# A longer distance between attention's matmuls and their operands in a planned schedule, with the steady part's ranks replaced

## The chip, the core and the metric

The kernel runs on one core of one Trainium2 chip. The metric is device time in microseconds, from repeated executions; one more execution is taken with the hardware profiler, and all rows below come from that one.

## What is computed

Attention with pooled keys and values, and behind it a feed-forward network with a PReLU. Cut to what matters:

```python
# q, k, v: (8, 8, 576, 64)   w_in: (512, 2048)   w_out: (2048, 512)   alpha: (2048,)
k_p = k.reshape(B, H, 72, 8, D).mean(axis=3)
v_p = v.reshape(B, H, 72, 8, D).mean(axis=3)
scores = np.matmul(q, k_p.transpose(0, 1, 3, 2)) / np.sqrt(D)
attn = softmax(scores)                      # over the 72 pooled keys
x = np.matmul(attn, v_p).transpose(0, 2, 1, 3).reshape(4608, 512)
h = x @ w_in
g = np.maximum(h, 0.0) + alpha * np.minimum(h, 0.0)
return g @ w_out
```

All of it is float32. The kernel forms each float32 product from float16 halves: an operand is scaled by a power of two and split into a high and a low part, and three matmuls (low x high, high x low, high x high) make one product.

## The kernel before

**Tiling.** The 4608 tokens go in nine chunks of 512 (c = 0 to 8). A chunk has attention (four tiles of 128 tokens), the first FFN matmul (FFN1, 512 to 2048 features), the PReLU, and the second (FFN2, 2048 to 512). Chunk 0 and attention of chunk 1 belong to the start, which has a plan and constants of its own (RK). The steady part follows: FFN of chunks 1 to 8 and, one chunk ahead of it, attention of chunks 2 to 8. FFN1 of chunk 1 is a plain product (lines 1339 to 1341). From chunk 2 on it is a Winograd form of Strassen's product (the function fast, line 1368): seven products in place of eight on sums of quarters, in four blocks d for each chunk, with three PSUM banks x, y and z that ACT (line 1384) and DVE (line 1388) empty into SBUF between the products. FFN2 is plain for chunks 1 and 2 (lines 1575 to 1577), and half Winograd from chunk 3 on (ffn2s, line 1481). DVE, ACT and GpSimd do the PReLU (lines 1325, 1327) and the splits into halves (lines 854, 857, and 1438 to 1450 for the sums that FFN2's products need; the step at 1450 gives back a buffer that the next copy of line 1384 takes).

**Attention of a chunk** (the function ahead). k, q and v are loaded by SP's DMA queue (lines 1028, 1039, 1076); DVE sums k and v over eight rows (1030, 1078). The largest absolute value gives a scale: reduce_max has ACT or GpSimd spread the partitions' maxima over a diagonal (lines 259 and 261), one small matmul bring them to all partitions (line 265, called the bring here), and DVE take the maximum. ACT and DVE split q, k and v. Then, for each of four tiles: a scores matmul (line 651), a maximum, a subtraction, an exponential, a sum and a reciprocal (1122 to 1127, 304, 306), GpSimd's multiplication (1131), copies into the padded tile apad (1133 to 1138), and a transposing DMA into aT (1142). After two tiles each comes a mix, the product with v (line 661), whose result is split into x (1169 to 1198). A chunk's first scores also wait for the first FFN1 block of the chunk before (gate). There is one S bank of PSUM, one e tile and one apad for all of it.

**What sets the order.** Every step is given to a planner, `_Plan.add`, with its engine, an estimated duration, the steps that it comes after, a rank, and the slots that it takes and gives (`take`, `give`: buffers and banks). `emit` simulates the engines in time and writes the instructions in the order found; each engine then runs its own in that order, and semaphores guard the data. A step may start, for the planner, when its engine is free, its slots are free, and its operands are there:

```python
t = [self.free.get(op["engine"], 0.0)]
t += [d["end"] + op["slack"] for d in op["after"] if self.loose < 1 or d["engine"] != op["engine"] or d["engine"] == "SP"]
```

So `slack`, the distance, is added to the end of each operand that another engine makes (loose is 1), and not to slots. The end of a step has 0.13 us added for the hop between engines, a DMA 2.0 (HOP, DMA_HOP). Of the steps of an engine that could start within a short time of the first (NEAR: 0.05 us on DVE, 0.18 on ACT, 0.37 on GpSimd, 0.07 on PE) the one with the lowest rank goes. A rank is 1000 times the chunk plus a constant of the table RB: `top` for the evacuations of Winograd's banks, `late`, `last`, `pr` and `gp` for PReLU and splits, `f1s`, `f2`, `f2s` and `f2o` for FFN products, and for attention `ld` (q), `k`, `v`, `t0` to `t3` (tiles), `x` and `y` (mixes). A name with `_` is the same for chunk 2. Attention of chunk c + 1 has 1000 c as its base, as the FFN of chunk c has.

The distances: 0.2 for attention's steps by default, FAR = 0.6 for its scores (line 1115), its mixes (line 1164) and the matmuls that sum weights (line 1242, whose operands are PE's own), 0.3 for Winograd products and 0.1 for plain FFN2 products. The bring has the default.

Of the kernel before, what the change touches and what calls it, by code (L numbers as in the profile page):

```python
# [56 lines left out]
def _new_b(c):  # L57
# [10 lines left out]
          ld1=13695.5, ld1s=7460.7, one=0, vl=6947.7, ld2=6076.4, q0=-19570.2, v0=1372.2, sm0=-8437.5,  # L68
          sms0=1712.0, mix0=-2376.7, q1=6121.6, v1=8243.2, sm1=3009.5, sms1=2826.1, mix1=16889.9)

RB = dict(gate=0, ld=4164.3, k=3254.6, v=4232.2, t0=-10914.8, t1=-12652.6, t2=-1841.8, t3=-12650.9, x=-4876.9,
          y=-10807.7, sum=-2021.0, pl=-18854.5, pp=5227.9, top=-10886.6, late=-13984.8, last=12811.0,
          pr=-12701.6, gp=11083.2, f2=7996.3, w1=-21973.2, sg=-4791.0, top2=-11574.2, f2o=1648.1, sum2=-1841.6,
          sums=1092.3, a2=-16165.4, ld_=1931.9, k_=-9571.1, v_=-13979.9, t0_=1665.0, t1_=-4791.7, t2_=-13992.2,
          t3_=2394.1, x_=-22301.6, y_=1604.9, sum2s=-10358.3, f2s=37.7, f1s=1612.4, out=2429.2)

# [103 lines left out]
def pooled_attention_prelu_ffn(ctx: ExitStack, tc: tile.TileContext, qT, kT, vT, vN, w1, w2, alpha, out):  # L182
# [14 lines left out]
    gp = ctx.enter_context(tc.tile_pool(name="gp", bufs=16))  # L197
# [34 lines left out]
    sg = const.tile([P, NF], F32, name="sg")  # L232
# [395 lines left out]
    last, scaled, pooled_v = {}, {}, []  # L628
# [331 lines left out]
    with tc.manual_schedule(engines={ENG.SP, ENG.PE, ENG.DVE, ENG.Activation, ENG.Pool}):  # L960
        plan = start()
# [24 lines left out]
        ld=[ldp.tile([P, KH], F32, tag="ld", name="ld") for _ in range(2)],  # L986
# [10 lines left out]
    def held(kind, tile_):  # L997
        box = _Box(kind)
        box.slot = tile_
        return box  # L1000
    add, FAR = plan.add, 0.6
    NQ = NF // 4
    pairs = lambda d: [(d, j) for j in range(2)]
    tw = {p: pieces[n] for n, p in enumerate(p for d in range(NS) for p in pairs(d))}
# [5 lines left out]
    def ahead(c, rank):  # L1010
        bs, n, at = _new_b(c), [0], ["ld"]

        def add(*a, **k):
            n[0] += 1
            return plan.add(*a, **{"slack": 0.2, **k, "rank": rank + RB[at[0] + "_" * (c == 2)] + 0.001 * n[0]})
        kss = {b: _Box("f", lambda t: t[:, :NPR * SP].rearrange("p (a s) -> p a s", s=SP)) for b in bs}
        m = once(lambda: sml.tile([P, 4], F32, tag="m", name="m"))
        e = once(lambda: sml.tile([P, 4], F32, tag="e", name="e", bufs=4))
# [6 lines left out]
        for j, b in enumerate(bs):  # L1025
            for i in range(2):
                t = _Box("ld")
                x = add("SP", 1.65, lambda i=i, b=b, t=t: nc.sync.dma_start(out=t(), in_=kT[b, :, i * KH:i * KH + KH]),
                        take=t)
                done.append(add("DVE", 1.3, lambda i=i, b=b, t=t: nc.vector.tensor_reduce(  # L1030
                    out=kss[b]().rearrange("p a s -> p (a s)")[:, i * KH // POOL:(i + 1) * KH // POOL],
# [6 lines left out]
        for i in range(2):  # L1038
            x = [add("SP", 1.46, lambda i=i: nc.sync.dma_start(out=q[i](), in_=qT[c, i]), *x, take=q[i])]
# [12 lines left out]
        for j, b in enumerate(bs):  # L1052
# [3 lines left out]
                out=kbs[b % 2][:, :, 1], in0=kss[b](), scalar=s()[:, j + 2:j + 3], in1=kbs[b % 2][:, :, 0],  # L1056
                op0=ALU.mult, op1=ALU.subtract), h, give=kss[b], two=True))
        for i in range(2):
            h = add("ACT", 1.13, lambda i=i: nc.scalar.activation(
                q16s[c][i]()[:, 0], q[i](), AF.Copy, scale=s()[:, 1 - i:2 - i]), sc)  # L1060
            for j in range(2):
                ps_ = slice(2 * j, 2 * j + 2)
                h = add("DVE", 0.7, lambda i=i, ps_=ps_: nc.vector.scalar_tensor_tensor(
                    out=q16s[c][i]()[:, 1, ps_], in0=q[i]()[:, ps_], scalar=s()[:, 1 - i:2 - i],
# [6 lines left out]
        for b in bs:  # L1071
            vs = _Box("f", lambda t: by_head(t[:SP]))
            ps = []
            for i in range(4):
                t = _Box("ld", lambda t: t[:SP, :2 * D * POOL].rearrange("p (a d w) -> p a d w", a=2, w=POOL))
                x = add("SP", 0.82, lambda i=i, b=b, t=t: nc.sync.dma_start(out=t(), in_=vT[b, :, 2 * i:2 * i + 2]),
                        take=t)
                ps.append(add("DVE", 1.15, lambda i=i, t=t, vs=vs: nc.vector.tensor_reduce(  # L1078
                    out=vs()[:, 2 * i:2 * i + 2, :], in_=t(), axis=AX.X, op=ALU.add), x, *ps[-1:],
# [5 lines left out]
            x = add("DVE", 0.65, lambda vm=vm, vs=vs: absmax(vm()[:SP], vs().rearrange("p h d -> p (h d)")), z, *ps)  # L1085

            def vscale(t, w, b=b, vsc=vsc):
# [3 lines left out]
            x = reduce_max(add, lambda vm=vm: vm(), 1, vscale, 0.3, x, home=_Box("S"))  # L1091
            x = add("ACT", 0.72, lambda v16=v16, vs=vs, vsc=vsc: nc.scalar.activation(
                v16()[:SP, 0], vs(), AF.Copy, scale=vsc()[:SP]), x, take=v16)
            y = add("DVE", 0.73, lambda v16=v16, vs=vs, vsc=vsc: nc.vector.scalar_tensor_tensor(
                out=v16()[:SP, 1], in0=vs(), scalar=vsc()[:SP], in1=v16()[:SP, 0],
                op0=ALU.mult, op1=ALU.subtract), x, give=vs, two=True)
# [8 lines left out]
        for i in range(TPC):  # L1105
# [7 lines left out]
            x = add("PE", 0.56 * len(_parts(c, i)), lambda i=i, ps=ps: scores(c, i, ps()), *kd,  # L1113
                    qd[2 * (i // 2) + 1], *tiles[-1:], *gate.get((c - 1, RB["gate"]), ()),
                    take=(ps, ex), give=q16s[c][i // 2] if i % 2 else (), slack=FAR)
# [4 lines left out]
            def top(i=i, mx=mx, sv=sv):  # L1120
                descale(c, i)
                nc.vector.tensor_reduce(out=mx(), in_=sv(), axis=AX.X, op=ALU.max)
            x = add("DVE", 0.9, top, x)
            x = add("DVE", 0.75, lambda ex=ex, mx=mx, sv=sv: nc.vector.tensor_tensor(
                out=ex(), in0=sv(), in1=mx().broadcast_to([P, 2, 4, SP]), op=ALU.subtract), x, give=ps, slack=0.0)
            x = add("ACT", 0.78, lambda i=i, ex=ex: nc.scalar.activation(ex(), ex(), AF.Exp, scale=descale(c, i)), x)
            x = add("DVE", 0.75, lambda sm=sm, ex=ex: nc.vector.tensor_reduce(
                out=sm(), in_=ex(), axis=AX.X, op=ALU.add), x)

            x = add("DVE", 0.4, lambda i=i: over9(i), x, slack=0.0)  # L1130
            x = add("Pool", 1.15, lambda ex=ex, sm=sm: nc.gpsimd.tensor_tensor(  # L1131
                out=ex(), in0=ex(), in1=sm().broadcast_to([P, 2, 4, SP]), op=ALU.mult), x)
            y = add("ACT", 0.68, lambda ev_=ev_: nc.scalar.copy(out=ap[:, 0, :, :SP], in_=ev_()), x, take="ap")  # L1133
            z = add("SP", 0.5, lambda: nc.sync.dma_start(out=ap[:, 1, :, :SP], in_=ap[:, 0, :, :SP]), y)
            x = add("Pool", 1.0, lambda ev_=ev_: nc.gpsimd.tensor_tensor(  # L1135
                out=ap[:, 0, :, SP:], in0=ev_()[:, :, :LO0], in1=ap[:, 0, :, :LO0], op=ALU.subtract), y)
            w = add("Pool", 0.45, lambda ev_=ev_: nc.gpsimd.tensor_tensor(
                out=ap[:, 1, :, SP:2 * SP - LO0], in0=ev_()[:, :, LO0:], in1=ap[:, 0, :, LO0:SP], op=ALU.subtract),
                y, x, give=ex, slack=0.0)
# [39 lines left out]
        ps, x = halves(0)  # L1179
# [4 lines left out]
        ps, x = halves(1)  # L1184
# [482 lines left out]
```

## Time and profile before

| | |
|---|---|
| median of 3 runs | 824.03 us (823.13 to 824.06) |
| the profiled execution | 823.68 us |
| its span, first to last instruction | 821.9 us |
| granted TensorE clock, mean | 0.994 of full speed |
| busy: DVE | 76% |
| busy: ACT | 58% |
| busy: GpSimd | 51% |
| moved by DMA | 137.98 MB, mean 168 GB/s |

How to read it: shares are of the span. PE is TensorE's matmuls; they are pipelined, so the time in which PE is busy contains the latency of each, and two matmuls that follow each other overlap. Steps of a chain of waits are the work that the end goes back to: each piece is what released the next one. A wait is the idle time of an engine just before an instruction, put down to what released it last. The start, up to about 150 us, includes most of PE's idle time; the steady part is what comes after it.

### The profile page before, as it was taken

The numbers are of one execution on the slowest core, as the hardware profiler recorded it, in microseconds if no ns is written. First come the engines' busy times: TensorE is split into PE (matmuls) and PEld (weight loads), VectorE is DVE, ScalarE is ACT, GpSimd is POOL, SyncE is SP. The second block draws the span as 40 slices with busy tenths as digits, with TensorE's granted clock in tenths as the row PEclk, the third lists the DMA queues.
The fourth block names the chain that finished last, engine by engine and source line by source line (L and its number), as shares of the span: only waits on it lengthen the run. The fifth ranks groups of instructions, "written<-read, shape, count | busy, mean of one in ns | idle before, by whom it ended". The sixth has DMA issues, their size and how long they took to land.

```text
span 821.9 us, 17523 instructions
## 1 busy us (share of the span) xinstructions
PE 788.3 (96%) x7075; PEld 593.4 (72%) x7075; DVE 627.2 (76%) x1070; ACT 480.6 (58%) x824; POOL 417.6 (51%) x412
## 2 busy tenths in 40 slices
PE   6889998989999989999999999999999999999998
PEld 4634444445458745788888888888888888888887
DVE  6999996599978966997799788978886587338710
ACT  5799874566356564566366736664575465526521
POOL 1657854246454554467455626563565365525430
PEclk9989999999999999999999999999999999999999
DMA  9994216447975984775487658674646164425001
GB/s 350 295 318 163 87 47 124 148 160 216 239 238 196 286 227 114 204 243 145 113 221 182 186 143 238 165 185 129 205 143 148 41 208 149 122 56 203 2 26 52
DMA packets 134833, 137.98 MB, mean 168 GB/s; under 512 B 108032, under 2 KB 111168, under 8 KB 134752
## 3 DMA queue, kind: packets, MB, share of 16 engines
q1 hardware_dynamic: 134752, 136.87, 57.3%
q8 instruction: 55, 0.90, 0.4%
q14 instruction: 26, 0.21, 0.1%
HBM read 96.48 MB, written 16.78 MB: 138 GB/s over the span
## 4 chain that ended last, share of the span: by engine, by line
PE 65%; DVE 15%; DMA 9%; ACT 5%; issue 3%; POOL 2%; DVEq 0%; ACTq 0%; POOLq 0%; SPq 0%
PE b L1368 25%; PE b L1481 23%; DMA aT<-apad 5%; PE b L1575 3%; PE b L1577 3%; PE b L1576 3%; PE s L651 1%; PE s L661 1%; DVE w L748 1%; DMA ld<-vT_dram 1%; DVE h L1327 1%; DVE v L720 1%; PE b L1339 1%; PE b L1341 1%; PE b L1340 1%
## 5 line engine op out<-in xcount | busy, mean ns | idle before, releaser
L1368 PE MATMUL b<-x,w 128*128 128x256 f16 x2352 | 271.4, 273 | 1.9 <-ACT h L1384 1.2
L1368 PEld LDWEIGHTS <-w 128*128 128x128 f16 x2352 | 228.4, 98 | 33.1 <-issue 2.1
L1481 PE MATMUL b<-w,g 128*128 128x256 f16 x1584 | 183.8, 273 | 0.6 <-ACT hw L1527 0.6
L1481 PEld LDWEIGHTS <-g 128*128 128x128 f16 x1728 | 168.1, 98 | 21.5 <-issue 1.7
L857 POOL TENSOR_TENSOR g<-h,g 128x512 f16<-128x512 f32 x88 | 107.4, 1232 | 78.1 <-ACT g L854 77.1
L1327 DVE SCALAR_TENSOR_TENSOR h<-h,al 128x512 f32<-128x512 f32 x88 | 73.8, 875 | 9.8 <-ACT h L1325 9.7
L1388 DVE TENSOR_TENSOR h<-b,h 128x512 f32<-128x512 f32 x85 | 58.0, 685 | 22.8 <-PE b L1368 22.1
L1325 ACT ACTIVATE h<-h,rp 128x512 f32<-128x512 f32 x78 | 52.2, 714 | 31.3 <-DVE h L1388 30.7
L854 ACT CAST g<-h 128x512 f16<-128x512 f32 x88 | 52.4, 616 | 20.3 <-DVE h L1327 10.6
L857 POOL TENSOR_TENSOR g<-hw,g 128x512 f16<-128x512 f32 x40 | 47.5, 1199 | 30.3 <-ACT g L854 21.7
L1131 POOL TENSOR_TENSOR e<-e,sum 128x576 f32<-128x576 f32 x28 | 34.4, 1227 | 44.2 <-DVE sum L306 44.0
L1135 POOL TENSOR_TENSOR apad<-e,apad 128x448 f16<-128x448 f32 x28 | 33.3, 1188 | 45.4 <-ACT apad L1133 43.8
L1575 PE MATMUL b<-w,g 128*128 128x512 f16 x128 | 48.6, 380 | 0.0
L1576 PE MATMUL b<-w,g 128*128 128x512 f16 x128 | 48.5, 379 | 0.0
L1577 PE MATMUL b<-w,g 128*128 128x512 f16 x128 | 48.5, 379 | 0.0
L1481 PEld LDWEIGHTS <-sw 128*128 128x128 f16 x396 | 38.6, 98 | 6.3 <-issue 1.7
L1384 ACT COPY h<-b 128x512 f32<-128x512 f32 x39 | 22.5, 578 | 34.4 <-PE b L1368 27.4
L1522 DVE TENSOR_TENSOR h<-b,h 128x512 f32<-128x512 f32 x26 | 17.6, 687 | 32.7 <-PE b L1481 32.5
L1078 DVE TENSOR_REDUCE f<-ld 72x128 f32<-72x1024 f32 x24 | 28.8, 1205 | 11.9 <-DMA ld<-vT_dram 11.8
L1388 DVE TENSOR_TENSOR hw<-b,hw 128x512 f32<-128x512 f32 x40 | 27.3, 684 | 10.6 <-PE b L1368 8.0
L1176 POOL TENSOR_TENSOR x<-h,x 128x512 f16<-128x512 f32 x16 | 19.5, 1230 | 28.7 <-ACT x L1169 28.6
L1481 PE MATMUL b<-sw,sw 128*128 128x256 f16 x264 | 33.0, 273 | 1.1 <-DVE hw L1540 1.1
(282 smaller groups left out, 1553.5 us busy)
## 6 DMA issues: line engine op xcount, KB each, us to landing
w<-b SPq DMA_DIRECT2D x56, 896.0 KB
w<-w_dram SPq DMA_DIRECT2D x16, 1024.0 KB
ld<-vT_dram SPq DMA_DIRECT2D x24, 288.0 KB
ld<-kT_dram SPq DMA_DIRECT2D x12, 576.0 KB
ld<-qT_dram SPq DMA_DIRECT2D x12, 512.0 KB
b<-w SPq DMA_DIRECT2D x8, 512.0 KB
out_dram<-h SPq DMA_DIRECT2D x16, 256.0 KB
apad<-apad SPq DMA_DIRECT2D x28, 144.0 KB
```

What stands on the lines that cost most here:

```text
L854: nc.scalar.copy(out=g[:, 0], in_=t)
L857: nc.gpsimd.tensor_tensor(out=g[:, 1], in0=t, in1=g[:, 0], op=ALU.subtract)
L1131: x = add("Pool", 1.15, lambda ex=ex, sm=sm: nc.gpsimd.tensor_tensor(out=ex(), in0=ex(), in1=sm().broadcast_to([P, 2, 4, SP]), op=ALU.mult ...
L1135: x = add("Pool", 1.0, lambda ev_=ev_: nc.gpsimd.tensor_tensor(out=ap[:, 0, :, SP:], in0=ev_()[:, :, :LO0], in1=ap[:, 0, :, :LO0], op=ALU. ...
L1325: nc.scalar.activation(t, t if src is None else src, AF.Copy, scale=rp[:, f:f + 1])
L1327: nc.vector.scalar_tensor_tensor(out=t, in0=t, scalar=al[:, f:f + 1], in1=t, op0=ALU.mult, op1=ALU.max)
L1368: nc.tensor.matmul(ps[:, q], weights(n, ws[q](), l, k), x[:, r, k], start=begin and not (q or k or e), stop=end and q + k + e == 4, skip_g ...
L1388: nc.vector.tensor_tensor(out=half(*o) if o else z, in0=banks[bank](), in1=z, op=ALU.add)
L1481: nc.tensor.matmul(bank[b]()[:, i], a, w, start=b in fresh, stop=stop, skip_group_check=True)
L1575: nc.tensor.matmul(ps, g[:, 1, ts_], w[:, 0, cs], start=(n == 0), stop=False)
L1576: nc.tensor.matmul(ps, g[:, 0, ts_], w[:, 1, cs], start=False, stop=False)
L1577: nc.tensor.matmul(ps, g[:, 0, ts_], w[:, 0, cs], start=False, stop=(n == NF - 1))
```

## The change

Three edits. The constant FAR goes from 0.6 to 1.8. The default distance of attention's steps stays 0.2 on all engines but PE, where it becomes 1.3; scores and mixes have FAR, so that on PE this is the bring of reduce_max. And the table RB has new values for all its 38 ranks (gate, the block whose end lets the next chunk's scores begin, stays 0). No operation is added or removed, and the start's constants stay.

```diff
-RB = dict(gate=0, ld=4164.3, k=3254.6, v=4232.2, t0=-10914.8, t1=-12652.6, t2=-1841.8, t3=-12650.9, x=-4876.9,
-          y=-10807.7, sum=-2021.0, pl=-18854.5, pp=5227.9, top=-10886.6, late=-13984.8, last=12811.0,
-          pr=-12701.6, gp=11083.2, f2=7996.3, w1=-21973.2, sg=-4791.0, top2=-11574.2, f2o=1648.1, sum2=-1841.6,
-          sums=1092.3, a2=-16165.4, ld_=1931.9, k_=-9571.1, v_=-13979.9, t0_=1665.0, t1_=-4791.7, t2_=-13992.2,
-          t3_=2394.1, x_=-22301.6, y_=1604.9, sum2s=-10358.3, f2s=37.7, f1s=1612.4, out=2429.2)
+RB = dict(gate=0, ld=1986.5, k=2080.0, v=2672.8, t0=-9490.5, t1=1792.0, t2=1603.8, t3=-13535.3, x=2823.5,
+          y=-342.4, sum=-2703.0, pl=880.9, pp=-4455.6, top=-1915.0, late=-3830.3, last=-1198.0, pr=-29472.6,
+          gp=2670.7, f2=9824.2, w1=1082.2, sg=-4068.9, top2=578.1, f2o=-1191.0, sum2=2688.9, sums=1785.4,
+          a2=-32370.0, ld_=10964.6, k_=1355.8, v_=-3660.6, t0_=-1142.8, t1_=-13646.8, t2_=5942.3, t3_=684.4,
+          x_=-13662.5, y_=1979.2, sum2s=-13639.8, f2s=2606.6, f1s=5636.5, out=-35531.5)
...
-    add, FAR = plan.add, 0.6
+    add, FAR = plan.add, 1.8
...
-            return plan.add(*a, **{"slack": 0.2, **k, "rank": rank + RB[at[0] + "_" * (c == 2)] + 0.001 * n[0]})
+            return plan.add(*a, **{"slack": 1.3 if a[0] == "PE" else 0.2, **k, "rank": rank + RB[at[0] + "_" * (c == 2)] + 0.001 * n[0]})
```

## Rows read from the trace of the kernel before

**Rows 1.** The page's busy times: each engine's busy us, share of the span, and instructions.

```profile
PE 788.3 (96%) x7075; PEld 593.4 (72%) x7075; DVE 627.2 (76%) x1070; ACT 480.6 (58%) x824; POOL 417.6 (51%) x412
```

**Rows 2.** Busy time by stretch from 150.2 us to the last matmul, seven stretches and their sum: the stretch and its length, busy us and instructions of PE, PEld (weight loads), DVE, ACT and POOL, the granted clock, the DMA engines' share and GB/s.

```profile
150.20:320.00 169.80, 164.56 (x1234) 96.78 (x1235) 135.97 (x242) 95.11 (x168) 88.37 (x84) 1.00 0.72 209
...
480.00:560.00 80.00, 80.00 (x834) 70.42 (x833) 67.73 (x112) 47.71 (x82) 44.42 (x43) 1.00 0.67 180
...
720.00:818.60 98.60, 97.95 (x902) 87.13 (x899) 44.32 (x70) 37.58 (x67) 31.39 (x28) 1.00 0.20 66
sum 668.40, PE 658.18 PEld 525.80 DVE 499.13 ACT 363.57 POOL 336.84; mean PE 94.03 PEld 75.11 DVE 71.31 ACT 51.94 POOL 48.12
```

**Rows 3.** Who waited for whom, PE alone, from 150.2 us on: us in total, times, the longest.

```profile
PE s L651 <- DVE x L1172: 2.7, 1, 2.7
PE s L265 <- ACT pd L259: 2.3, 1, 2.3
PE s L661 <- DMA aT<-apad: 1.5, 2, 1.3
PE b L1368 <- ACT h L1384: 1.2, 1, 1.2
PE b L1481 <- DVE hw L1540: 1.1, 1, 1.1
PE b L1481 <- ACT hw L1527: 0.6, 1, 0.6
PE b L1339 <- ACT o L873: 0.5, 1, 0.5
...
```

**Rows 4.** The chain of waits from 155 to 172 us: start, us, what.

```profile
157.69 4.00 DMA ld<-vT_dram
...
164.93 1.14 DVE f L1078
...
166.88 0.41 ACT pd L259
...
167.34 0.22 PE s L265
```

**Rows 5.** The chain of waits from 290 to 306 us.

```profile
294.85 7.07 DMA ld<-vT_dram
...
301.95 1.22 DVE f L1078
303.17 0.67 DVE x L1172
...
303.88 0.56 PE s L651 x24
```

**Rows 6.** Who waited for whom, DVE alone, from 150.2 us on, the row of v's loads.

```profile
DVE f L1078 <- DMA ld<-vT_dram: 11.8, 6, 5.4
```

**Rows 7.** The chain of waits from 376 to 397 us.

```profile
386.36 2.84 DMA apad<-apad
...
389.26 5.20 DMA aT<-apad
...
394.60 1.08 PE s L661 x16
```

**Rows 8.** PE's instructions in order of time, at seven places asked for one by one (a short window can cut a group, so that the start and the idle time in brackets are what counts): start, us, instruction and shapes, number, idle time before and what ended it.

```profile
274.53 0.72 PE L1368 MATMUL b<-x,w 128*128 128x256 f16 x5 [0.22 <-DMA w<-b]
...
319.55 0.52 PE L661 MATMUL s<-aT,v 88*64 88x256 f16 x6
...
403.58 0.40 PE L651 MATMUL s<-kb,q 64*128 64x72 f16 x14
...
449.08 1.14 PE L1368 MATMUL b<-x,w 128*128 128x256 f16 x9 [0.31 <-DVE h L1388]
...
598.75 0.38 PE L1368 MATMUL b<-x,w 128*128 128x256 f16 x2 [1.24 <-ACT h L1384]
...
648.02 0.47 PE L651 MATMUL s<-kb,q 64*128 64x72 f16 x18
...
659.76 0.43 PE L651 MATMUL s<-kb,q 64*128 64x72 f16 x16
```

**Rows 9.** The scores line, L651, in four short windows around the first scores of chunks 5 to 8: matmuls, their ns at least, in the middle and at most, first and last start.

```profile
L651 PE MATMUL s<-kb,q x24: 195/195/203, 403.6 to 403.9; 64*128 64x72 f16 x24
...
L651 PE MATMUL s<-kb,q x24: 195/195/203, 484.4 to 484.8; 64*128 64x72 f16 x24
...
L651 PE MATMUL s<-kb,q x24: 195/195/203, 565.4 to 565.8; 64*128 64x72 f16 x24
...
L651 PE MATMUL s<-kb,q x24: 195/195/203, 648.0 to 648.4; 64*128 64x72 f16 x24
```

**Rows 10.** The page's DMA issues: what is moved, number, KB each.

```profile
w<-b SPq DMA_DIRECT2D x56, 896.0 KB
...
ld<-vT_dram SPq DMA_DIRECT2D x24, 288.0 KB
```

**Rows 11.** SP's issues in order of time before the load of 294.85: start, us of the issue, what, number.

```profile
290.49 0.99 SPq L1357 DMA_DIRECT2D w<-b  x2
```

**Rows 12.** The chain of waits from 590 to 600 us.

```profile
596.47 1.62 POOL sw L1450
...
598.11 0.60 ACT h L1384
```

## The prediction

> **What bounds the kernel now.** I read the page first: TensorE (PE) is busy 96% of the span and every other engine 76% or less [rows 1]. Then the stretches of the span. From 150.2 us, where chunk 1's FFN begins and the order comes from the ranks that the diff rewrites, to the last matmul at 818.6, PE is busy 658.18 of 668.40 us, at a granted clock of 1.00 in every stretch (the upper of its two levels, 2.4 GHz) [rows 2]. So the changed part is PE-bound, its matmuls are the same before and after, and all that a new order can win there is the 10.2 us in which PE is idle. What lies before 150 us has an order of its own, with constants that the diff leaves alone.
>
> Then the list of PE's waits in that part shows who holds those 10.2 us [rows 3]. Attention's own matmuls wait 6.5 us: one scores matmul 2.7 (line 651), one of the small matmuls that spread a maximum over the partitions 2.3 (line 265; I call it the bring), two mixes 1.5 (line 661). FFN matmuls wait nearly all of the rest, on bank evacuations by DVE and ACT and on a weight load.
>
> Last I followed the chain of waits back from the three long ones. The bring of chunk 2 waits for ACT, that for a maximum on DVE, that for a sum over v whose load was issued at 157.69 and took 4.00 us to land [rows 4]. The scores matmul at 303.88 waits for a DVE step that stood behind another such sum, whose load took 7.07 us [rows 5]. DVE as a whole lost 11.8 us to these loads in six places [rows 6]. The mix at 394.60 waits for the DMA transpose of its second half, 5.20 us in the chain behind a copy of 2.84 [rows 7].
>
> **The change part by part.** FAR goes from 0.6 to 1.8 and the default distance of attention's PE steps from 0.2 to 1.3. A distance only tells the planner to treat an operand as ready so much later; it adds no instruction and no wait on the chip. It counts for operands of other engines alone (the start method skips operands from the step's own engine), and not for slots (`take`). That decides where it acts:
>
> - The 14 mixes take transposes (SP) and v (DVE, SP): they get 1.2 us more. The two waits that the list gives as 1.5 together are 1.28 (the marked one at 394.60) and the rest, 0.2. 1.2 us more distance takes 1.2 and 0.2: **-1.4**. Bounds: 0, if the planner had put the mix there for its rank and not for its operand, to -1.5. Nothing is late behind it: PE's next wait comes at 449.08 and is 0.31 [rows 8].
> - The 13 brings get 1.1 us more, as their default is the 1.3. One waits, 2.3: **-1.1**. Bounds 0 and -2.3. PE's next wait behind it comes at 274.53, 0.22 [rows 8].
> - The scores: of the four tiles of a chunk only those with fresh k or q have operands of another engine near; the others wait for the slots S and e, for which no distance counts. The one wait of 2.7 is for the slot S, given back by line 1172: **0**. Bounds 0 and -2.7.
> - The weight sums' matmuls have FAR too, but their listed operands are PE's: nothing.
>
> What a later mix costs on PE: nothing as long as FFN products stand ready to go before it, and they do: from 480 to 560, with eight scores and mixes among them, PE is busy 80.00 of 80.00 us [rows 2]. What it costs along attention's loop: a chunk's first scores wait for the FFN of the chunk before to begin, and that for the mixes before it. First scores start at 403.6, 484.4, 565.4 and 648.0 [rows 9], 80.8, 81.0 and 82.6 us apart, which is what PE needs for a chunk, since it hardly idles there. The loop's own pieces are shorter: two tiles' scores as close as 11.7 us (648.02 to 659.76), so 35.2 for three; last scores to last mix 15.7 (303.88 to 319.55); last mix to the next first scores 9.0 (394.60 to 403.58) [rows 5, 7, 8]. Sum 59.9, some 21 us below 81. The change adds 2 x 1.2 for mixes and at most 4 x 1.2 for scores, 7.2. With that cover the cost is 0; without it up to 7.2 in each of the six loops, 43 us.
>
> The third part is the search: all 38 ranks are new. They choose which of the steps ready within a few hundredths to a few tenths of a microsecond goes first, on every engine, so they draw all waits of rows 3 anew and not only attention's. No row shows the new order. Bounds: if every stretch ran like 480 to 560, the 10.2 us would go; if every stretch ran like 150.2 to 320 (idle 5.24 of 169.80, 3.1%), idle time would be 668.4 x 0.031 = 20.6, which is 10.4 more. I take **0**, since the mean stretch lies between, with as many waits as now that aren't attention's operands.
>
> Sum: -1.4 - 1.1 = -2.5. The profiled execution took 823.68, its span 821.9; 823.68 - 2.5 = 821.2. The median of the runs, 824.03, lies 0.35 above it: **821.5 us**, 0.3% below the median.
>
> A rule on the root of the two longest waits. The two v loads took 4.00 and 7.07 us from issue to use [rows 4, 5]; the second, of 288 KB, was issued 4.4 us behind two weight blocks of 896 KB [rows 10, 11]. The Trainium skill (SBUF — State Buffer, The DMA setup-cost knee) gives a transfer about 2 us fixed and its bytes at 436 GB/s; for 288 KB that makes an estimate of 2.7 us. The trace doesn't agree here: both loads were slower. By the rule a lone load would be in time, and an order that leaves these loads alone would do without both waits; by the trace, loads that meet weights and transposes don't.
>
> **The rivals.**
>
> *The search moves the v loads out of the way.* Then the bring's wait and the scores' both go, 2.3 + 2.7 = 5.0 in place of the 1.1: 821.5 - 3.9 = 817.6, and with some of the FFN's waits less. For it: the chains of rows 4 and 5 have one root, and v's rank is among those rewritten (4232.2 to 2672.8, and for chunk 2 -13979.9 to -3660.6). Against: the ranks of k and q loads move in the same direction, so the traffic around v needn't thin, and the planner's 0.82 us and hop of 2.0 for such a load are unchanged, 1.2 below the shorter of the two durations seen and 4.3 below the longer.
>
> *No net gain.* The 2.5 us are won and the new ranks lose as much on other waits, or the covered waits were never the last: PE arrives earlier at the next bank that isn't free. 824.0. For it: 7.7 of the 10.2 us are waits that a distance doesn't reach. Against: the covered ones are followed by FFN products without idle time, so the time won isn't given back at once.
>
> *Slower: bank evacuation falls behind attention.* In the Winograd blocks (28 of them, four for each of chunks 2 to 8) the next product waits for ACT's copy (line 1384) or DVE's sum (line 1388) of its bank. One such wait shows its price: at 598.75 PE idles 1.24 us for ACT's copy, which itself had waited for GpSimd's step at line 1450 to give back the buffer that it writes [rows 8, 12]. The rank of these evacuations goes from -10886.6 to -1915.0, that of attention's tiles 0 and 3 stays at -9490.5 and -13535.3, so these two now go ahead of it by thousands where they went ahead by 28 and 1764 before. Against: tile 1 went ahead too and now goes behind (1792.0), and the wait that gives the price was a buffer's and not attention's doing. From the fourth additional wait (4 x 1.24 = 5.0 against 2.5 + 1.65 = 4.2) the kernel is slower than the bound of no change; with five it is 821.5 + 5 x 1.24 = 827.7, and ten, the worst stretch's rate, would give about 834.
>
> *Slower: the loop binds.* If the 21 us of cover aren't there, since DVE does FFN work between attention's steps, some loops grow by up to 7.2: two of them give 836. Against: loops with 80 us that PE filled.
>
> **How the numbers follow.** About 0.2%, 1.65 us, is what a measurement of this kernel can tell from no change: below 822.4 is faster, above 825.7 slower. The forecast's own case, waits covered and the rest about as many as now, reaches from 817.6 to 822.4 and gets 0.40. The v loads out of the way, 817.6 down to 814.1 (the floor, 824.03 less 10 us), get 0.13. No net gain, 822.4 to 825.7, gets 0.21. Evacuation behind attention gets 0.24 and the loop 0.02. Faster is 0.40 + 0.13 = 0.53, the same 0.21, slower 0.26. The range goes from 815.0, leaving out the last microsecond above the floor (some 0.03), to 829.0, which holds the slower case up to six more waits and leaves out the dearer part and the loop (some 0.13). The forecast's own range beside it is 817.6 to 822.4.
>
> **What would show it.** Right: line 661 has no wait on the transposes over 0.3 us, line 265 none over 1.3; the granted clock stays at 1.00; first scores of chunks 5 to 8 stand about 81 us apart; idle time of PE from 150 us on falls from 10.2 to about 7.7. Waits of line 651 on slots remain of the size of 2.7. The v rival: line 1078 waits far less than 11.8 us for its loads. The evacuation rival: lines 1368 and 1481 wait over 8 us in place of 3.4 for lines 1384, 1388, 1522, 1527 and 1540. The loop: first scores over 84 us apart and a long idle stretch before a chunk's first FFN product. The prediction is wrong if idle time of PE doesn't fall, or if it falls without line 661 and line 265 having any part in it.

## The result, and the profile after

| | before | after |
|---|---|---|
| median of 4 runs each, same chip | 824.04 us (823.13 to 825.12) | 834.50 us (832.97 to 835.02) |
| ratio | 1 | 1.0109 [1.0088, 1.0130] |
| the profiled execution, its span | 823.68, 821.9 us | 834.53, 832.8 us |

The change makes the kernel 1.1% slower: 10.5 us in the medians, 10.9 in the spans. The forecast was 821.5, and its range ended at 829.0.

I read the profile of after in the order of the prediction. The page's busy times, beside [rows 1]:

```profile
PE 793.2 (95%) x7075; PEld 594.8 (71%) x7075; DVE 635.1 (76%) x1070; ACT 480.1 (58%) x824; POOL 422.5 (51%) x412
```

Every engine has the same number of instructions. PE is busy 4.9 us longer with the same 7075 matmuls, so some of them ran slower. The stretches of the span show where, beside [rows 2] (one stretch is added at the end, since the last matmul now ends at 829.5; the columns are those of rows 2):

```profile
150.20:320.00 169.80, 159.48 (x1191) 94.05 (x1189) 142.50 (x242) 95.14 (x168) 86.96 (x84) 0.98 0.74 207
...
480.00:560.00 80.00, 79.27 (x827) 69.48 (x825) 67.25 (x112) 48.36 (x85) 44.30 (x43) 1.00 0.68 188
...
720.00:818.60 98.60, 97.06 (x894) 86.42 (x893) 45.46 (x72) 36.93 (x65) 35.01 (x32) 1.00 0.19 63
818.60:830.00 11.40, 10.29 (x93) 8.82 (x91) 1.14 (x3) 3.19 (x6) 0.00 (x0) 1.00 0.23 81
sum 679.80, PE 661.71 PEld 526.47 DVE 508.51 ACT 363.47 POOL 340.97; mean PE 82.71 PEld 65.81 DVE 63.56 ACT 45.43 POOL 42.62
```

From 150.2 us to the last matmul it is 679.3 us where before had 668.4. PE idles 679.3 - 661.7 = 17.6 us in place of 10.2, and is busy 3.5 us longer. Two thirds of the new idle time (10.3 in place of 5.2 us) are in the first stretch, 150 to 320, which is also the only one with a granted clock below 1.00.

PE's waits, beside [rows 3] (us in total, times, the longest):

```profile
PE b L1368 <- DMA w<-b: 3.8, 1, 3.8
PE b L1368 <- ACT hw L1384: 2.4, 2, 1.5
PE b L1368 <- DVE h L1388: 2.3, 3, 1.3
PE b L1339 <- ACT h L1325: 2.1, 1, 2.1
PE b L1368 <- ACT h L1384: 1.3, 2, 0.7
PE b L1368 <- POOL x L1176: 1.1, 1, 1.1
PE b L1339 <- ACT hw L1325: 1.1, 1, 1.1
PE s L651 <- DVE x L1172: 1.0, 1, 1.0
...
PE s L265 <- DVE e L1124: 0.2, 1, 0.2
```

Attention's own matmuls waited 6.5 us before and wait 1.2 now: the mixes (line 661) are gone from the list, the bring (265) has 0.2 in place of 2.3, the scores (651) 1.0 in place of 2.7. That is 5.3 us, more than the 2.5 that I gave the distance. What came in their place is all FFN, whose waits in this list went from 3.5 to 16.1 us: a weight load that is late by 3.8, banks that ACT and DVE had not emptied (lines 1384, 1388), and plain FFN1 products of chunk 1 waiting for PReLU (1325). DVE's waits for v's loads fell as well, from 11.8 [rows 6]:

```profile
DVE f L1078 <- DMA ld<-vT_dram: 7.0, 4, 2.1
```

**The largest loss.** The chain of waits from 236 to 275 us leads to it, then PE's and ACT's instructions in order of time (idle time before them, and what ended it, in brackets), then four short stretches with the granted clock in the column before the last two:

```profile
252.00 1.37 PE b L1368 x11
253.37 8.12 DMA w<-b
261.49 0.05 issue
261.54 8.47 PE b L1368 x54
```

```profile
261.54 8.47 PE L1368 MATMUL b<-x,w 128*128 128x256 f16 x54 [3.76 <-DMA w<-b]
...
263.70 0.69 ACT L1581 ACTIVATE o<-b,os 128x512 f32<-128x512 f32 x1 [6.06 <-DMA out_dram<-o]
```

```profile
250.00:255.00 5.00, 3.86 (x52) 2.87 (x50) 5.00 (x7) 3.54 (x8) 4.58 (x4) 1.00 1.00 360
...
261.00:263.00 2.00, 1.46 (x7) 1.03 (x8) 0.26 (x1) 0.00 (x0) 0.00 (x0) 0.50 0.30 97
263.00:265.00 2.00, 2.00 (x11) 1.44 (x10) 0.00 (x0) 1.30 (x3) 0.00 (x0) 0.50 0.00 1
265.00:267.00 2.00, 2.00 (x13) 1.52 (x12) 0.69 (x1) 1.72 (x4) 0.88 (x1) 0.62 0.76 236
```

PE stands still for 3.76 us for a block of Winograd weights of chunk 2 (896 KB, issued at 253.37 and landed 8.12 us later; from 250 to 255 the DMA engines were busy throughout, at 360 GB/s). Behind the wait PE runs at the lower of its two levels, 1.2 GHz, until some 5 us later: the 54 matmuls take 8.47 us where 54 such matmuls take 5.9 at the upper level (60 of them take 6.55 us in e17 below). So the one late load costs 3.76 + 2.6 = 6.4 us at its place, in this execution. And at the same place ACT is blocked 6.06 us on the store of an output tile, of which more below.

**Three copies behind output stores.** At 492.95, 688.54 and 765.03 PE waits 0.64, 0.89 and 1.48 us for ACT's copy of a bank (line 1384). The chain from 756 to 766 shows why, and the releasers of line 1384 give the sum (the line has no such row in the kernel before):

```profile
760.06 4.24 DMA out_dram<-hw
764.40 0.59 ACT hw L1384
765.03 1.03 PE b L1368 x8
```

```profile
  DMA out_dram<-hw: 4.8, 2
  DMA out_dram<-h: 0.9, 1
```

ACT's copy writes into an SBUF buffer whose last content is still being stored to memory, until 4.24 us after the store was issued.

### The profile page after: what moved, and what is told of

Its sections match the earlier page's. It is cut to its first block, busy times and chain, and to the rows that moved or that the text cites. A ratio compares the mean times of both kernels' runs of the same rounds, so it can differ in the third digit from the quotient of the medians.

```text
span 832.8 us, 17521 instructions
## 1 busy us (share of the span) xinstructions
PE 793.2 (95%) x7075; PEld 594.8 (71%) x7075; DVE 635.1 (76%) x1070; ACT 480.1 (58%) x824; POOL 422.5 (51%) x412
## 4 chain that ended last, share of the span: by engine, by line
PE 60%; DVE 23%; DMA 7%; ACT 5%; issue 4%; POOL 1%; DVEq 0%; ACTq 0%; POOLq 0%; SPq 0%
PE b L1481 25%; PE b L1368 24%; DMA aT<-apad 2%; DVE h L1327 2%; PE b L1575 2%; PE b L1577 2%; PE b L1576 2%; DMA w<-b 2%; PE s L651 1%; PE s L661 1%; DVE w L748 1%; DVE v L720 1%; DMA out_dram<-hw 1%; DVE vw L717 1%; DVE h L1388 1%
## 5 line engine op out<-in xcount | busy, mean ns | idle before, releaser
L1368 PE MATMUL b<-x,w 128*128 128x256 f16 x2352 | 274.1, 274 | 11.2 <-DMA w<-b 3.8
L857 POOL TENSOR_TENSOR g<-h,g 128x512 f16<-128x512 f32 x88 | 110.1, 1263 | 75.3 <-ACT g L854 70.6
L1327 DVE SCALAR_TENSOR_TENSOR h<-h,al 128x512 f32<-128x512 f32 x88 | 77.0, 911 | 13.7 <-ACT h L1325 13.4
L1388 DVE TENSOR_TENSOR h<-b,h 128x512 f32<-128x512 f32 x85 | 58.1, 685 | 32.2 <-PE b L1368 29.8
L1176 POOL TENSOR_TENSOR x<-h,x 128x512 f16<-128x512 f32 x20 | 25.1, 1270 | 58.7 <-ACT x L1169 58.7
L1388 DVE TENSOR_TENSOR hw<-b,hw 128x512 f32<-128x512 f32 x43 | 29.5, 686 | 13.7 <-PE b L1368 13.2
L1327 DVE SCALAR_TENSOR_TENSOR hw<-hw,al 128x512 f32<-128x512 f32 x40 | 34.0, 881 | 4.0 <-ACT hw L1325 4.0
L1126 ACT ACTIVATE e<-e,ds 128x576 f32<-128x576 f32 x28 | 21.6, 773 | 26.0 <-DVE e L1124 26.0
L1446 POOL TENSOR_TENSOR sw<-w,sw 128x256 f16<-128x256 f32 x18 | 13.4, 745 | 41.2 <-ACT sw L1445 38.2
```

Of the source, the lines that this page charges most:

```text
L857: nc.gpsimd.tensor_tensor(out=g[:, 1], in0=t, in1=g[:, 0], op=ALU.subtract)
L1327: nc.vector.scalar_tensor_tensor(out=t, in0=t, scalar=al[:, f:f + 1], in1=t, op0=ALU.mult, op1=ALU.max)
L1368: nc.tensor.matmul(ps[:, q], weights(n, ws[q](), l, k), x[:, r, k], start=begin and not (q or k or e), stop=end and q + k + e == 4, skip_g ...
L1388: nc.vector.tensor_tensor(out=half(*o) if o else z, in0=banks[bank](), in1=z, op=ALU.add)
```

## The experiments

The ratios are against the kernel before, run beside it on the same chip (medians 823.96 to 826.46). The planner's own end is the time at which its simulation finishes; it is arithmetic and no measurement: 800.6 for the kernel before and 803.7 for the one after. So by that arithmetic the new order was 3.1 us longer already, and the chip added 21.3 and 29.1 to it in the spans.

### One half of the change at a time

e1, the distances alone on the kernel before:

```diff
-    add, FAR = plan.add, 0.6
+    add, FAR = plan.add, 1.8
...
-            return plan.add(*a, **{"slack": 0.2, **k, ...})
+            return plan.add(*a, **{"slack": 1.3 if a[0] == "PE" else 0.2, **k, ...})
```

> The two distances (1.8 and 1.3) with the ranks of the kernel before. Theory A (the distances help, the new ranks cost the time): the waits of lines 265 and 661 go, faster than before by 1 to 4 us, 820 to 823, and TensorE never drops to 1.2 GHz after 150 us. Theory B (the longer distances push attention's steps into the way of bank evacuation and weight loads, and the ranks have little part): slower than before by 5 us or more, 829 to 835.

e2, the ranks alone, which is the kernel after with 0.6 and 0.2:

```diff
-    add, FAR = plan.add, 1.8
+    add, FAR = plan.add, 0.6
...
-            return plan.add(*a, **{"slack": 1.3 if a[0] == "PE" else 0.2, **k, ...})
+            return plan.add(*a, **{"slack": 0.2, **k, ...})
```

> The new ranks with the distances of the kernel before (0.6 and 0.2). Theory A: all of the loss and the waits that the distances had saved, 835 to 841, with waits on line 1384 and 1388 of some 7 us and attention's waits back. Theory B: about the time of the kernel before, 822 to 827.

e1 took 838.98 us, 1.0151 [1.0130, 1.0172]; e2 861.11, 1.0419 [1.0388, 1.0449]. Both halves alone are slower than the whole, and slower than either theory had them. PE's longest waits and those of attention, first of e1, then of e2:

```profile
PE b L1575 <- DVE sw L1256: 7.6, 1, 7.6
PE b L1368 <- DVE h L1388: 3.5, 5, 1.7
PE b L1368 <- DMA w<-b: 1.9, 1, 1.9
...
PE s L265 <- DVE e L1124: 0.3, 1, 0.3
PE s L661 <- DMA aT<-apad: 0.3, 1, 0.3
PE s L265 <- DVE x L1172: 0.3, 1, 0.3
```

```profile
PE s L661 <- DMA aT<-apad: 11.2, 6, 5.8
PE b L1368 <- ACT h L1384: 7.6, 2, 5.6
PE b L1368 <- DMA w<-b: 3.6, 2, 2.5
PE s L651 <- DVE q L1063: 3.1, 2, 2.8
```

The two lists part what the distances do to attention's waits from what the ranks do. With the distances alone they fall from 6.5 to 0.9 us; with the ranks alone they rise to 14.3. So the new ranks by themselves take none of them away.

With the old ranks the distances redraw the order so that a plain FFN2 product waits 7.6 us for a sum over weights of the Winograd blocks (line 1256). With the new ranks and the old distances the mixes wait 11.2 us for their transposes: the planner takes these as there 2 us after their issue has ended, and PE, which comes by that reckoning, finds them late. So the four cells are 1.0000 (old, old), 1.0151 (distances new), 1.0419 (ranks new) and 1.0109 (both). The distance takes 3% off within the new ranks and adds 1.5% within the old. The whole isn't a sum of two effects.

### Is it the distance as such, or one rank?

e6, a mild distance on the kernel before, where the planner's own end hardly changes:

```diff
-    add, FAR = plan.add, 0.6
+    add, FAR = plan.add, 0.9
```

> The kernel before with FAR = 0.9 and nothing else, a distance at which the planner's own end is nearly that of before (802.4 for 800.6). Theory A (the chip's time is the planner's end plus what the chip is late against it, and a distance by itself costs next to nothing): within 5 us of the kernel before, mix waits smaller than before's 1.5. Theory B (a longer distance costs time as such): 5 us slower or more.

825.64 us, 1.0012 [0.9990, 1.0034]: no difference. These 0.3 us more cost nothing. Nor did they shorten the waits of the mixes: 3.1 us in four places, where before had 1.5. (By the planner's arithmetic FAR = 0.9 ends at 802.4; e1's full distances end at 815.9 with the old ranks, 15.3 us later than before.)

e3 and e4 give single late ranks of the new table their old values, w1 in e3, and top and pl, the evacuations that my slower rival blamed, in e4; e5 moves the weight sums 385 ahead:

```diff
-  ... w1=1082.2, ...            e3
+  ... w1=-21973.2, ...
-  ... pl=880.9, ... top=-1915.0, ...            e4
+  ... pl=-18854.5, ... top=-10886.6, ...
-  ... sums=1785.4,            e5
+  ... sums=1400.0,
```

> The changed kernel with one rank of before, w1 = -21973.2, that of the loads of weight blocks (line 1357). If that rank put the block load that PE waited for at 261.5 us behind other issues: no wait on w<-b over 0.5 us, a granted clock of 1.00 after 150 us, and 6 to 8 us less than the changed kernel, 826 to 829. If the late load has another cause (a slot that comes free late, traffic of other transfers): the wait of 3.8 and the stretch at 1.2 GHz stay, 833 to 836.

> The changed kernel with two ranks of before, top = -10886.6 (evacuation of the Winograd banks, lines 1384 and 1388) and pl = -18854.5 (that of the plain product's banks, line 1325). If these ranks made the evacuations late: waits of lines 1368 and 1339 on ACT and DVE fall from some 11 us to 4 or less, and the time by 6 to 10 us, 824 to 829. If DVE is late there for other reasons (in-order work with long steps, whatever the rank): waits as in the changed kernel, 832 to 837.

> The changed kernel with the constant sums at 1400.0 in place of 1785.4, so that the planner puts the last pair's weight sums and their store earlier (its plan has the last store 4.7 us earlier and the fourth weight block load 5.0 us earlier). If PE's wait of 3.8 at 261.5 us and the clock's drop behind it come from that store: the last store (line 1261) is issued before 244 us, the wait on w<-b is under 0.5 and the granted clock stays at 1.00 up to 300 us. If the load is late for another reason: the wait and the drop stay. The total says little, since the planner draws the rest of its order anew and its own end is 19 us later (822.8 for 803.7): 840 to 860 either way.

All three are slower than after: 848.77 us, 1.0256 [1.0222, 1.0291]; 853.88, 1.0330 [1.0296, 1.0363]; 853.25, 1.0337 [1.0302, 1.0373]. In e3 the wait for the weight load stays, at 4.2. In e4 the waits for line 1384, which the old rank should have taken away, are the longest of all, 8.9 us in five. In e5 (two runs) the load wait is gone, but the sums' last store went out at 247.5, half a microsecond earlier than in after, where 4 us were expected, and three other waits of 7.0, 6.8 and 3.4 came; the run says nothing on its cause. A single rank moved draws the whole order anew, so this way of undoing the change one part at a time doesn't isolate anything: the rank of the evacuations isn't shown to be guilty, and I had blamed it.

### Other ranks, and a planner told that DMAs take longer

e7 has the new distances with a third set of 38 ranks. e8 to e12 tell the planner that a DMA takes longer (DMA_HOP), which is closer to the 4 to 8 us from issue to landing that the rows show, each with ranks of its own:

```diff
-    HOP, DMA_HOP = 0.13, 2.0
+    HOP, DMA_HOP = 0.13, 4.0      e8, e10 (distances 0.6, 0.2)
+    HOP, DMA_HOP = 0.13, 3.0      e9 (0.9, 0.3)
+    HOP, DMA_HOP = 0.13, 2.5      e11 (0.9, 0.3)
+    HOP, DMA_HOP = 0.13, 3.5      e12 (1.8, 1.3)
...
-RB = dict(gate=0, ld=4164.3, k=3254.6, v=4232.2, ...)
+RB = dict(gate=0, ld=3241.0, k=2470.7, v=3422.3, ...)      e8
```

> The distances 1.8 and 1.3 with a third set of ranks, started from those of before and moved to where the planner's own end is 807.9 (before 800.6, changed kernel 803.7, the distances with the ranks of before 815.9). Theory A: 829 to 835 on the chip where the kernel before takes 824, waits of lines 265 and 661 under 0.5 each. Theory B: 838 or more, as with the ranks of before. If a set of ranks that is worse in the plan than that of the changed kernel is faster on the chip, the plan doesn't see what makes the changed kernel slow.

> The distances of before (0.6 and 0.2), with the planner's hop of a DMA at 4.0 in place of 2.0 for the steady part, and ranks moved to where the planner's own end is least with that (814.7, of which the longer hop is a part). If late DMAs (weight blocks, stores, v) are what is left of the loss: no wait of PE on a DMA or behind one over 1 us, granted clock 1.00 all through, and the chip's time nearer to the planner's end than in any other kernel (before: 23.5 above it), 826 to 834. If DVE's and ACT's order is what is left: waits of lines 1368 and 1481 as in the changed kernel, 836 or more.

> Distances 0.9 (FAR) and 0.3, the planner's DMA hop 3.0 in place of 2.0 in the steady part, ranks moved to where the planner's own end is 808.3. Theory C (what separates the chip from the plan is late DMAs, and a distance at DMA results is worth more than one at PE's operands): nearer to the plan than the kernel before by 5 to 9 us, within 5 us of it in time, no wait of PE on w<-b over 1. Theory D (any new set of ranks is late elsewhere by as much): 828 or more with before at 824, and waits on DVE and ACT of over 10 us.

> As e8 (hop 4.0, distances 0.6 and 0.2) with ranks moved further: planner's own end 813.5 in place of 814.7. Theory C: 1 us faster than e8, some 0.4% slower than the kernel before, its end on the chip 12 to 14 us above the planner's. Theory D: a scatter of 5 us or more against e8.

> Distances 0.9 and 0.3, hop 2.5, planner's own end 806.6. Theory C: between the kernel before (23 us above its plan) and e9, 825 to 829. Theory D: 830 or more.

> The change's distances, 1.8 and 1.3, with the hop at 3.5, planner's own end 818.5. Theory C: the change's two large late DMAs don't come back (no wait on w<-b over 1 us, no bank copy behind an output store), the chip 11 to 14 us above the plan, 830 to 834, as fast as the changed kernel though its plan is 15 us longer. Theory D: 838 or more.

| | us | ratio | PE's longest wait |
|---|---|---|---|
| e7 | 832.04 | 1.0082 [1.0055, 1.0109] | line 1575 for the sums of line 1256, 6.3 |
| e8 | 829.32 | 1.0053 [1.0035, 1.0071] | line 1368 for ACT's x (1169), 2.6 |
| e9 | 831.94 | 1.0095 [1.0074, 1.0115] | line 1575 for 1256, 6.5 |
| e10 | 831.14 | 1.0086 [1.0069, 1.0103] | line 1368 for ACT's x (1169), 2.6 |
| e11 | 826.14 | 1.0012 [0.9994, 1.0031] | mix for its transpose, 1.7 |
| e12 | 846.63 | 1.0286 [1.0249, 1.0323] | line 1575 for 1256, 6.8 |

e7 says that the plan's end doesn't order the kernels: its plan ends 4 us later than after's, and it isn't slower. e8 did take the waits on DMAs out of PE's list, and the chip came nearer to the plan, as expected (a span of 827.5 for a plan of 814.7), but the plan itself is 14 us longer, and waits on DVE and ACT grew (1388 3.9, 1540 3.0). e12 is the clearest: it has the change's distances, no load wait over 0.2 us and no bank copy or scaling behind a store, all as expected, and takes 846.63 in place of the 830 to 834 that went with that. Telling the planner of longer DMA times gave nothing faster than the kernel before in five tries; the one that equals it, e11, has the mildest values. So an order without those waits is to be had in this way, but it brought others, as far as these sets of ranks can tell.

### The order kept, one suspected wait taken away

What did isolate was to keep the order of every engine as it is in after and to take away what a wait was for.

e13: the second half of chunk 2's Winograd block 1 takes its weights from a tile that is in SBUF already, so that the late load isn't waited for (its values are not those that the block needs).

```diff
-    nc.tensor.matmul(ps[:, q], weights(n, ws[q](), l, k), x[:, r, k],
+    nc.tensor.matmul(ps[:, q], weights(n, ws[q]() if (c, d, q) != (2, 1, 1) else wraw[2, 6]()..., l, k), x[:, r, k],
```

> The changed kernel, every engine's order kept, where chunk 2's block 1 takes half of its weights from a tile of w2 that lies in SBUF all along, and not from the block whose load came late (that load is still issued; chunk 2's result is another). Theory E (the waits that the changed kernel shows are worth their length and, for the long one, the clock that it costs): the wait of 3.8 at 261.5 goes, TensorE stays at a granted clock of 1.00 from 255 to 270 us, and the time falls by 3.9 + 2.6 = 6.5 us, to some 0.3% to 0.5% above the kernel before. Theory F (the next late step takes the wait's place): the time falls by less than 2 us and a wait on DVE or ACT appears within 15 us.

e14: the output stores of line 1532 left out in chunks 3 to 7; e15 is the control, the same on the kernel before; e16 has the edits of e13 and e14 together.

```diff
-    add("SP", 0.8, lambda: nc.sync.dma_start(out=out[t0:t0 + P, cs], in_=R[h]()[:, i, cs]), *after, ...)
+    add("SP", 0.8, lambda: nc.sync.dma_start(out=out[t0:t0 + P, cs], in_=R[h]()[:, i, cs]) if done else None, *after, ...)
```

> The changed kernel, every engine's order kept, without the output stores of chunks 3 to 7 (the last chunk's stay, and those of chunks 0 to 2). Theory E: the three bank copies (line 1384) that stood behind a store go through, PE's waits of 0.64, 0.89 and 1.48 with them, the time falls by 3.0 to 3.5 us. Theory F: under 1 us, since DVE's sums of the same banks (line 1388) are late next.

> The kernel before without the same stores. Theory E: no change beyond 1 us, since none of PE's waits there lies behind a store. If it falls by 3 us as well, the stores' traffic slows something else, and what e14 gains isn't the bank copies' doing.

> The changed kernel with both: weights of that half block from the tile in SBUF, and no output stores of chunks 3 to 7. Theory E: the two add up, 9.5 to 10 us less than the changed kernel, within 0.2% of the kernel before. Theory F: not more than the larger of the two.

e13: 833.62 us, 1.0113 [1.0082, 1.0145], no gain. e14: 831.21, 1.0081 [1.0050, 1.0111]. e15: 824.85, 1.0005 [0.9987, 1.0023]. e16: 830.46, 1.0061 [1.0035, 1.0087], and not the 9.5 to 10 us less that the two were to add up to.

The stores are nearly as expected. The order is the same, so the start of each matmul can be set against that of the same matmul in after. By that e14 gains 0.8, 1.05 and 1.64 us at the three places, 3.5 together (2.3 us in the ratios, whose intervals overlap), and the control gains nothing: before, no copy stood behind a store. e14's profile, its fastest run, has 3 us more than that over after, all before 267 us: there the wait for the late load was 1.7 us and the clock stayed at 1.00, though the first store left out would have come at 435. So the 6.4 us of the load aren't fixed by the order; they differ from one execution to the next.

The load is the miss that taught most. Set against after in the same way, e13 gains 6.3 us between 248.6 and 266.6 and has given 4.5 of it back by 276; the rest is less than the ratios can tell. (It had lost 1.7 at 180, where its clock dropped and after's didn't.) Its waits, its stretches and its chain from 255 to 272 say how:

```profile
PE b L1575 <- POOL g L857: 2.6, 1, 2.6
```

```profile
180.00:185.00 5.00, 5.00 (x17) 1.97 (x16) 5.00 (x7) 5.00 (x10) 1.62 (x1) 0.66 0.19 61
...
272.00:276.00 4.00, 3.92 (x19) 2.46 (x18) 3.20 (x6) 1.39 (x2) 1.90 (x3) 0.59 1.02 235
```

```profile
256.49 8.16 DMA out_dram<-o
264.75 0.04 ACT o L1581
265.34 0.58 ACT h L1384
267.09 0.63 ACT h L1325
```

The late work that takes the load's place is ACT's. FFN2's result of chunks 1 and 2 goes through the single tile o: ACT scales it (line 1581), SP stores it (1585), and the next scaling waits for the store. In after the rank `out` went from 2429.2 to -35531.5, the lowest constant of the table, which puts the scaling ahead of anything else that ACT could do at that time; it then stands at the head of ACT's queue until the store has landed, here 8.16 us after its issue (ACT idles 5.60 of them), with PReLU's steps for FFN2 behind it. No run gave that rank alone its old value. In before this line never waited for a store; in after its releasers read

```profile
  DMA out_dram<-o: 7.5, 2
```

e17 tests that: e16's edits, and the eight stores of o left out; e18 is its control, both kinds of stores left out of the kernel before.

```diff
-            nc.sync.dma_start(out=out[t0:t0 + P, cs], in_=o()[:, cs])
+            nc.sync.dma_start(out=out[t0:t0 + P, cs], in_=o()[:, cs]) if done else None
```

> The edits of e13 and e14 together, and in addition the eight stores of ffn2's output o of chunks 1 and 2 (line 1585) left out, so that their part of the output is not written; the order of the work is kept. Theory F (ACT was blocked 6.1 us at 263.7 behind the store of the only o buffer, and that is the late work which took the place of the load wait in e13 and e16): ACT is not blocked at line 1581, line 1575's wait of 2.6 us on g (line 857) and the clock below 1.00 at 272 to 276 go, so the profile has 4 to 5 us less than the one of e16, and the time against before falls from 1.006 to about 1.000 to 1.002. Theory G (what is late there is the vector engine's and GpSimd's own work, the store only seems to hold it): the wait at line 1575 stays over 1.5 us and the time stays within 1.5 us of e16's, at 1.005 to 1.007.

> Control: the kernel before without the same stores (line 1532 in chunks 3 to 7, line 1585 in chunks 1 and 2, that part of the output not written). Both theories: no wait of the kernel before was on one of these stores, so within 1.5 us of it, 0.998 to 1.001. If it were 4 us faster, the gain of e17 would be the DMA traffic's and not the blocked engine's.

e17: 826.71 us, 1.0012 [0.9997, 1.0027]. e18: 826.69, 1.0011 [0.9996, 1.0027]. PE's longest waits in e17, its first stretch, and its chain at the place of the late load:

```profile
PE b L1339 <- ACT h L1325: 2.1, 1, 2.1
PE b L1368 <- DVE h L1388: 1.7, 2, 1.3
PE b L1368 <- DMA w<-b: 1.3, 1, 1.3
PE s L651 <- DVE x L1172: 1.0, 1, 1.0
```

```profile
150.20:320.00 169.80, 163.63 (x1232) 96.23 (x1231) 146.41 (x246) 96.50 (x172) 87.47 (x85) 1.00 0.73 206
```

```profile
256.64 6.55 PE b L1368 x60
```

The wait at line 1575 is gone, the clock is 1.00 in all of the first stretch, and the time is that of the kernel before, with after's order on every engine. Set against after matmul by matmul, e17 gains 6.7 us between 248.6 and 266.6, loses 1.5 at 274 to 280 on a later weight load (1.3 in the list), and gains 3.8 at the three copies: 9.0 us. Up to 248.6 the two executions stand level, and the spans are 10.0 apart (832.8 and 822.8). The three kinds of stalls on transfers, load, output stores and the store of o, are therefore what made the kernel slower than before. From e16 to e17 the intervals don't overlap, so the store of o has a part of its own; the load's part isn't separated, as no run leaves out o's stores and keeps the load's wait. Leaving out stores also thins the traffic, which by e15 and e18 gains nothing in the order of before; in after's order this wasn't tried by itself.

Without the stalls after's order is as fast as before's and no faster: attention's waits are 1.2 us there in place of 6.5, but FFN's are 8.1 in place of 3.5. So the gain on attention is given back, stalls or no stalls.

No edit here is a version to keep, since e13 to e18 leave out or change part of the computation, and no version that computes all of it was faster than the kernel before.

## Why the prediction was wrong

- **What bounds the kernel**: right. The steady part is PE-bound, with the same matmuls, and what was lost is idle time of PE and clock, not work.
- **"-1.4" for the mixes and "-1.1" for the bring**: right in kind, and reached in full: the mixes' wait is gone (1.5 before), the bring's fell by 2.1. **"0" for the scores** was too low: 2.7 became 1.0. The gain on attention is 5.3 us, not 2.5. e1 has it with the old ranks (0.9 us of attention's waits left) and e2 doesn't with the new ones (14.3), so it is the distances'; but e7, with the same distances and other ranks, keeps 4.0. No distance counts for the slot that the scores waited for, so there it is the redrawn order; how was not looked at.
- **The loop at 0**: right. First scores of chunks 5 to 8 start at 411.6, 497.0, 574.8 and 657.3 in after, 85.4, 77.8 and 82.5 apart. One gap is over the 84 that I named, but no long wait of PE goes with it: none from 400 to 560 is over 0.64 us.
- **The new ranks: "I take 0, since the mean stretch lies between"**: this is the step that failed. Its size is the loss in all and what the distance won beside it: 10.9 + 5.3 = 16.2 us, of which the stalls on transfers are some 10 (the spans of after and e17), and most of the rest smaller FFN waits that e17 has too. The bounds that I gave ended at 10.4. Two things were wrong in it. First, the upper bound was taken from idle time only (the worst stretch's 3.1%), and a stall also costs clock: 2.6 of the 6.4 us at 261. Second, I took the redraw as neutral, since waits come and go; but the order of the kernel before had no PE wait over 0.3 us on a load, and none of its copies or scalings stood behind an output store. A new order is free to spoil that: to the planner a transfer has ended 2 us after its issue has ended, and the stores that held the buffers landed 4.2 to 8.2 us after theirs began.
- **Rival, no net gain (0.21)**: missed in its number, and yet what e17 shows once the stalls are out: attention's waits won, as much lost on others. The reason that I gave against it, that FFN products follow the covered waits without idle time, was read from the old order.
- **Rival, evacuation behind attention (0.24)**: right on the side and partly on the lines (1384, 1388), wrong on the reason. The waits that I named as its sign are 7.7 us, just under the 8 (and 3.3 before, where I wrote 3.4). 3.0 of them are copies behind an output store, in three places (e14, e15): a copy waiting for its buffer, which I had used as the price and set aside as "a buffer's and not attention's doing". Nothing shows the rank `top` guilty: its old value, with that of `pl`, made these waits longer (e4).
- That ten more waits at my price "would give about 834", which is what was measured, is chance: these waits grew by 4.5 us, and most of the loss came in another way.
- **Rival, v loads out of the way (0.13)**: its sign came true, DVE's waits for v fell from 11.8 to 7.0, without paying, as FFN's waits took more than that.
- **The signs that I named**: line 661 has no wait, line 265 none over 1.3, both as said, and first scores lie 81.9 us apart on average; the idle time of PE didn't fall to 7.7 but rose to 17.6, and the clock didn't stay at 1.00. The first two show the steps on the distance right, the last two the sum wrong.

Open: why e5's earlier rank for the sums hardly moved their store, what the load is worth by itself, and which ranks put the copies behind the stores and the weight load late (for the store of o it is argued from the rank `out`, not shown). Only the transfers were shown to hold them.

## What to carry to other kernels

Where a written order is redrawn by a search, a priced gain on one kind of wait says little: ask first which engine could now stand, in order, behind a step that waits for a transfer to give a buffer back, and what the transfers of that place take in the trace. Take such waits out one at a time with the order kept, since moving a single rank changes everything else too. And when the longest wait is taken away and nothing is won, look at the other engines' queues at the same place: another may have been as late.

## What the runs showed of the hardware

- **The late load cost twice.** The 3.8 us wait at 261 was followed by 5 us at 1.2 GHz, which cost another 2.6. In e14's profile the same wait was 1.7 us and was followed by a granted clock of 1.00, and so was the 1.3 in e17. The clock isn't repeated exactly either: the wait of 2.1 us at 178 was followed by 1.00 from 180 to 185 in after and by 0.66 in e13, the same instructions in the same order.
- **Landing times in traffic.** A store of 256 KB took 4.2 to 5.6 us at the three copies and 8.16 at o in e13, and a weight block of 896 KB 8.12 us. None of them was alone: while they were under way the DMA share was 0.80 (the store of 4.24 us), 0.89 (4.67), 0.65 (5.55), 0.64 (8.16) and 0.77 (the weight block). The longest didn't have the highest share, so the share alone doesn't give the time, and a transfer by itself wasn't measured.
